# FFN bias added on GpSimd instead of TensorE, and FFN squares in place and two tiles wide, in a two-layer transformer kernel on one core

## The chip, the core and the metric

The kernel runs on one core of a Trainium2 chip. The metric is device time in microseconds. One execution of each kernel was also recorded by the hardware profiler. The engines are named as the profile names them: PE (TensorE, with PEld for its weight loads), ACT (ScalarE), DVE (VectorE), POOL (GpSimd) and SP (SyncE, which issues most DMAs here).

## The reference

Two layers with shared weights. Each is an attention and a feed-forward network (FFN), both behind a layer norm without parameters and with a residual. S = 2048 rows, D = 448, 16 heads of 28, F = 1792, all in bf16.

```python
def _A_ref(x, wqkv, wo):            # attention, 16 heads of 28, no mask
    q, k, v = split(x @ wqkv)
    p = softmax(q @ k.T * 28 ** -0.5)
    return (p @ v) @ wo

def _B_ref(x, w1, b1, w2, b2):      # FFN with a squared relu
    h = x @ w1 + b1
    r = where(h > 0, h, 0)
    return (r * r) @ w2 + b2

x = A_x
x = x + _A_ref(_layernorm(x), A_wqkv, A_wo)
x = x + _B_ref(_layernorm(x), B_w1, B_b1, B_w2, B_b2)
x = x + _A_ref(_layernorm(x), A_wqkv, A_wo)
x = x + _B_ref(_layernorm(x), B_w1, B_b1, B_w2, B_b2)
```

(Cut and abridged; `_layernorm` subtracts the mean and divides by the root of variance plus 1e-5.)

## The kernel before

All weights and x stay in SBUF for the whole run. Rows are worked on in **blocks** of two row tiles of 128 (256 queries); in layer 1 the last two blocks have one row tile each. The list `blocks` holds them.

**Attention.** For a block and a group of four heads, scores are computed in **units** of 512 columns: keys times queries, one head each, four heads side by side in PE's rows. There are 2048 units. `s_stream` takes up to three units at a time into one PSUM tile `sc` of three banks (L1154). There are two such tiles. `e_stream` takes the exponential of a whole tile on ACT (L1192), as bf16 into one of twelve `pt` tiles; an instruction has 1536 columns, or 1024 when the third unit is taken out. A unit that is taken out (`apart`, `a_unit`) has its exponential worked out by integer arithmetic: DVE reads the scores (L1214 or L1216), then three steps follow on POOL or DVE (`bent` L1263, `half` L1269, `whole` L1274) and one product on DVE (`close` L1278). In the other form, `a_whole` (L1232 to L1239), everything is on DVE. `p_stream` multiplies the results with the values (tile `oT`, L1380 and L1345). The denominators come out of the same product, and `norm_pair` or `norm_turn` divides by them.

**After attention** of a block, `chain(l, qb)` runs: the product with `wo` and the residual (`add_to_x`, L1513), the layer norm (statistics L648, a power on POOL at L673, normalized rows L772, transposes on PE L712, copy to `xnT` L724), and the FFN. The FFN's first product makes `mt` tiles of 512 columns in PSUM: two chunks of 128 hidden values by 256 rows, seven tiles to a block of two row tiles. `relu` (L1582 on ACT, L1584 on DVE) reads the tile and writes a buffer `r`, of which there are two (`rp`, resource `R_r`); `square` (L1589, L1591) reads `r` and writes the hidden values to their place (`hidden`: parts of `K_sb[1]`, `Q_sb`, `V_sb` or a tile `h`). While exponentials remain, DVE does both; after the last one ACT may take relus, and squares of the block before the last (`aside`). The second product, with `w2`, starts with a matmul of `one0` (ones in row 0 and zeros elsewhere) and `b2w` (the bias b2 in row 0), which adds the bias. DVE adds the sum to `x_sb` (L1513). The two blocks of one row tile at the end of layer 1 (`late`) do without that matmul: POOL adds b2 to their rows into a buffer `xf` (L1555), from a copy of b2 that a late DMA has put on all partitions. In layer 0 the block then makes its keys, values and queries for layer 1; in layer 1 the rows are stored (L1612).

**Order.** Nothing is ordered by the compiler. A `Planner` runs while the kernel is built: streams yield `Op`s with planned durations and dependencies, and the planner always issues the one that can start first, with priorities and rules on top. So the order on each engine is fixed at build time, by constants. `PACE` sets such constants anew at certain score tiles; the tables `FORCE` and `SKIP` name score tiles at which a unit must or must not be taken out. Where PE has room, a score tile's matmuls are repeated (`MORE`, `HOT`), and `heat` puts in matmuls without use (L1641), to keep PE's load up. An Op with `port=True` is planned so that POOL and DVE take turns: a POOL Op of that kind starts after DVE's, and the other way round.

Of the kernel before, what the change touches and what calls it, by code (L numbers as in the profile page):

```python
# [11 lines left out]
DT = mybir.dt  # L12
AF = mybir.ActivationFunctionType
ALU = mybir.AluOpType
P = 128
# [23 lines left out]
XMIN = 4  # L39
HELD = 0.14  # L40
# [105 lines left out]
FORCE = (22, 27, 31, 36, 64, 104, 108, 120, 122, 156, 162, 192, 196, 233, 235, 237, 254, 263, 287, 292, 301, 306,  # L146
         329, 341, 392, 408, 430, 445, 466, 501, 515, 553, 556, 567, 577, 593, 598, 602)
SKIP = (20, 29, 46, 135, 184, 195, 216, 222, 242, 262, 280, 282, 320, 321, 378, 388, 395, 404, 406, 409, 416, 418,
        433, 440, 446, 479, 500, 512, 526, 544, 574, 601, 609, 621, 622, 646, 652, 663)
PACE = {  # L150
    0: {'BUSY': 0.95, 'LOW': 0.7, 'CHUNK': 1, 'EV': 2.9, 'FAR': 6, 'KEEP': 5, 'LAG': 8, 'LEAD': 18, 'MARGIN': 3,
         'MORE': 3, 'PRE': 0.5, 'SLACK': 0.7, 'SPAN': 8, 'TB': 2.4, 'TB2': 2.4, 'V_AGE': 5, 'V_LAST': 3, 'V_PAST':
# [3 lines left out]
    8: {'LEAD': 12, 'BUSY': 0.9, 'PLIM': 2},  # L156
    16: {'SPAN': 11},
    24: {'LAG': 3},
    32: {'PLIM': 2.6, 'EV': 3.5},
    40: {'TB2': 3.0},  # L160
    42: {'BUSY': 0.95, 'CHUNK': 3, 'EV': 2.9, 'LAG': 8, 'LEAD': 18, 'MORE': 1, 'SPAN': 8, 'TB': 1.6, 'TB2': 2.4,
         'V_PRIO': 8.5},
    56: {'BUSY': 1.0, 'LAG': 3},
    64: {'NEAR': 9, 'ASIDE': 0.2, 'LADD': 0.1},
    72: {'V_AGE': 4},
    88: {'V_AGE': 3},
    112: {'C_PRIO': 1.2, 'HOLD': 5},
    120: {'LEAD': 10, 'LAG': 12, 'SPARE': 3, 'ASIDE': 2},
    128: {'TB': 2.0, 'MORE': 3},
    136: {'PRE': 1.2, 'MARGIN': 6},  # L170
    144: {'EPRIO': 4},
    152: {'CHUNK': 1, 'VGAP': 0},
    160: {'BUSY': 0.95, 'V_PRIO': 4, 'V_PAST': 3},
    168: {'RES': 1, 'C_PRIO': 2.1, 'LOW': 1.0},
    176: {'EV': 2.2, 'TB2': 2.0, 'LOW': 0.5},
    192: {'PORTP': 0.3, 'SOON': 0.6},
    200: {'CHUNK': 2, 'PRE': 0.3},
    208: {'PNEAR': 0.25, 'V_AGE': 6},
    216: {'NEAR': 3},
    248: {'EPRIO': 6},  # L180
    256: {'ASIDE': 0},
    264: {'MARGIN': 10},
    280: {'PORTP': 2},
    288: {'HOLD': 6},
    296: {'TB': 1.0, 'PNEAR': 0.15},
    304: {'SPAN': 6},
    312: {'BUSY': 1.0},
    320: {'LEAD': 12, 'MARGIN': 6},
    328: {'V_LATE': 6},
    336: {'LOW': 1.0},  # L190
    360: {'PNEAR': 0.05, 'TB': 2.4, 'V_LATE': 2.6, 'V_AGE': 3},
    368: {'C_PRIO': 1.6},
    376: {'PNEAR': 0.15, 'V_PRIO': 8.5},
    384: {'XMIN': 3, 'LEAD': 18},
    392: {'CHUNK': 3},
    400: {'KEEP': 6, 'ASIDE': 4, 'V_AGE': 6, 'BUSY': 0.9},
    408: {'PWAIT': 0.6, 'MORE': 1},
    424: {'RES': 2, 'BUSY': 1.0},
    440: {'HEAT': 0.6, 'WINDOW': 3.4, 'CHUNK': 2},
    456: {'V_AGE': 5, 'TB': 1.3},  # L200
    480: {'TB': 1.6, 'PORTP': 0.3, 'PLIM': 2},
    488: {'LADD': 0.2, 'HOLD': 4},
    496: {'MARGIN': 3, 'PNEAR': 0.35},
    504: {'PWAIT': 0.3},
    512: {'KEEP': 4, 'EV': 2.9},
    520: {'V_AGE': 4, 'C_PRIO': 1.2, 'HOLD': 5},
    528: {'PRE': 0.8},
    536: {'XMIN': 4, 'SPAN': 15, 'ASIDE': 2, 'PRE': 0.3},
    544: {'V_AGE': 5, 'EV': 2.2},
    552: {'PORTP': 1, 'LEAD': 12, 'FAR': 17, 'PRE': 0},  # L210
    560: {'V_LATE': 6, 'VGAP': 0.03},
    568: {'SPARE': 0, 'NEAR': 9},
    576: {'SOON': 1.5, 'PNEAR': 0.15},
    584: {'PLIM': 1.3, 'LAG': 3, 'V_WAIT': 3},
    592: {'KEEP': 6, 'V_LAST': 2.2},
    600: {'V_AGE': 8},
    608: {'EV': 1.3, 'LOW': 0.8},
    616: {'PRE': 1.2, 'BUSY': 0.95, 'V_PAST': 2, 'FAR': 6},
    624: {'LADD': 0.1, 'BUSY': 0.9},
    648: {'PRE': 0.5, 'SPAN': 20, 'EV': 3.5, 'ASIDE': 0.2},  # L220
    656: {'ASIDE': 1, 'SLACK': 0.4},
    672: {'SOON': 1, 'ASIDE': 0.2},
    680: {'SLACK': 0.7},
# [183 lines left out]
def kernel(  # L407
# [45 lines left out]
    R_r, R_xt, R_os, R_xn, R_on, R_rec = Res(2), Res(2), Res(NOS), Res(2), Res(2), Res(2)  # L453
# [96 lines left out]
    def loads():  # L550
# [28 lines left out]
        yield dma(b2w[0:1, :], B_b2.rearrange("(o d) -> o d", o=1), 30 * kb, ("b2",))  # L579
# [937 lines left out]
    def chain(l, qb):  # L1517
# [30 lines left out]
        if late:  # L1548
            b2b = flat_of(K_sb[0])[:, S:S + D]
            if ("b2b",) not in pl.tok:  # L1550
                yield dma(b2b, B_b2.rearrange("(o d) -> o d", o=1).to_broadcast([P, D]), 112 * 1024, ("b2b",))
            xf = flat_of(K_sb[0])[:, 2 * D * (late - 1):2 * D * late].bitcast(DT.float32)

            def add(e):
                nc.gpsimd.tensor_tensor(out=xf, in0=x_sb[:, t0, :], in1=b2b, op=ALU.add)  # L1555
# [6 lines left out]
        def hidden(i):  # L1562
            flat = lambda a: a.rearrange("p (f q) -> p f q", q=n)
            if l == 0 and i < 4:
                return (K_sb[1], Q_sb)[i // 2][:, 2 * (i % 2):2 * (i % 2) + 2, t0 * P:t0 * P + n]
            if l == 0 and i < 6:
                return flat(V_sb[1][:, t0:t0 + nt, :, :].rearrange("p t h r -> p (t h r)")[:, QB * (i - 4):QB * (i - 3)])
            if l == 0:
                return flat(hp.tile([P, QB], DT.bfloat16, name="h")[:, :])

            c = NFC * QR * (own_h.turn % 2) + QB * i
            return flat(V_sb[0][:, :, :, :].rearrange("p t h r -> p (t h r)")[:, c:c + QB])
        for f0 in range(0, NFC, pack):
# [3 lines left out]
            b = {}  # L1577

            def relu(e, t, b=b, w=w):
                r = b["r"] = rp.tile([P, QB], DT.bfloat16, name="r")  # L1580
                if e == "ACT":
                    nc.scalar.activation(out=r[:, 0:w], in_=t[:, 0:w], func=AF.Relu)  # L1582
                else:
                    nc.vector.tensor_scalar(out=r[:, 0:w], in0=t[:, 0:w], scalar1=0.0, scalar2=None, op0=ALU.max)  # L1584
            def square(e, b=b, w=w, f0=f0):
                r = b["r"][:, 0:w].rearrange("p (f q) -> p f q", q=n)
                b["h"] = h = hidden(f0 // pack)
                if e == "ACT":
                    nc.scalar.activation(out=h[:, 0:w // n, :], in_=r, func=AF.Square)  # L1589
                else:  # L1590
                    nc.vector.tensor_tensor(out=h[:, 0:w // n, :], in0=r, in1=r, op=ALU.mult)  # L1591

            def then(o, b=b, square=square):
                aside = not s_left and (l, qb) == (1, len(blocks[1]) - 2)
                b["s"] = Op("ACT" if aside else "DVE", 0.5 if aside else 0.42, square, deps=[o], rel=o, port=True)
# [99 lines left out]
```

## Time and profile before

| | us |
|---|---|
| median of 3 runs (lowest to highest) | 803.51 (803.49 to 803.66) |
| the profiled execution, own time | 803.48 |
| its span, first to last instruction | 801.7 |
| first exponential starts | 9.28 |
| last exponential ends | 787.08 |

The profile gives a busy time for each engine, groups of instructions by line and shape (count, busy time, mean duration, and the idle time ahead of them with what ended it), a timeline with start and duration, and busy times in windows. Durations on ACT include a start-up and drain that overlap with the instruction next to them, and matmuls overlap too, so busy times of ACT and PE cannot be added up from single durations; the distance between two starts is the measure there. The granted TensorE clock was 1.00 throughout.

### The profile page before, as it was taken

Reading aid. Unit: us, or ns where it says so; the run is one execution under the profiler, and the core shown is the slowest. Engines: PE = TensorE matmul, PEld = TensorE weight load, DVE = VectorE, ACT = ScalarE, POOL = GpSimd, SP = SyncE. Lnnn points to the kernel's source line nnn. Section 1 sums busy time; section 2 is a strip of 40 time slices with the busy share of each in tenths; the row PEclk is TensorE's granted clock in tenths of the full one; section 3 lists DMA queues with packets and bytes.
Section 4 is the critical chain, followed back from the end, with each engine's and each line's share of the span. In section 5 each row is a group of like instructions: output and inputs, shape, how many; then the busy total and the mean of one; then the engine's idle time right before and its main releaser. Section 6 shows DMA issues by size and latency. Waiting matters only on the chain.

```text
span 801.7 us, 29246 instructions
## 1 busy us (share of the span) xinstructions
PE 778.7 (97%) x12242; PEld 417.6 (52%) x12242; DVE 744.8 (93%) x1818; ACT 789.4 (98%) x702; POOL 454.7 (57%) x717
## 2 busy tenths in 40 slices
PE   9999989999999999999999999989999999999998
PEld 6555545544555545555455545445454544545666
DVE  8999999999999999999999998999999999989564
ACT  8999999999999999999999999999999999999995
POOL 3346777657676664544566657657665566654200
PEclk9999999999999999999999999999999999999999
DMA  9300010000000000000000000011100000000100
GB/s 250 86 2 2 5 34 23 17 16 16 17 3 16 16 16 16 3 16 15 2 3 2 3 2 2 15 32 30 33 11 22 21 28 21 22 23 9 27 8 19
DMA packets 32480, 18.13 MB, mean 23 GB/s; under 512 B 17818, under 2 KB 31899, under 8 KB 32348
## 3 DMA queue, kind: packets, MB, share of 16 engines
q1 hardware_dynamic: 32204, 16.16, 7.4%
q8 instruction: 95, 1.56, 0.8%
q14 instruction: 37, 0.30, 0.1%
q10 hardware_dynamic: 144, 0.11, 0.0%
HBM read 13.98 MB, written 2.06 MB: 20 GB/s over the span
## 4 chain that ended last, share of the span: by engine, by line
PE 41%; ACT 33%; DVE 17%; issue 8%; DMA 0%; POOL 0%; ACTq 0%; DVEq 0%
ACT pt L1192 33%; PE mt L809 19%; PE sc L1154 12%; PE oT L1380 7%; DVE pt L1216 2%; DVE r L1584 2%; PE oT L1345 1%; DVE pt L1214 1%; DVE V_sb L1591 1%; DVE K_sb L1278 1%; DVE v_c L1278 1%; DVE v_c L1216 1%; PE tp L712 1%; DVE x_sb L1513 1%; PE sc L809 1%
## 5 line engine op out<-in xcount | busy, mean ns | idle before, releaser
L1192 ACT ACTIVATE pt<-sc 128x1536 bf16<-128x1536 f32 (+1 forms) x683 | 776.6, 1292 | 1.2 <-PE sc L1154 0.9
L1154 PE MATMUL sc<-Q_sb,K_sb 32*128 32x256 bf16 (+1 forms) x4652 | 279.6, 265 | 15.7 <-ACT pt L1192 13.5
L1154 PEld LDWEIGHTS <-K_sb 32*128 32x128 bf16 x4652 | 101.1, 92 | 186.3 <-issue 118.3
L1380 PE MATMUL oT<-pt,V_sb 128*32 128x256 bf16 (+1 forms) x4000 | 167.8, 268 | 0.5 <-DVE Q_sb L828 0.3
L1380 PEld LDWEIGHTS <-V_sb 128*32 128x32 bf16 x4352 | 101.5, 96 | 45.3 <-issue 35.9
L809 PE MATMUL mt<-xnT,w 128*128 128x256 bf16 (+1 forms) x904 | 119.6, 270 | 0.9 <-DVE xnT L724 0.2
L1274 POOL TENSOR_SCALAR pt<-pt 128x512 int16<-128x512 int8 x131 | 83.9, 642 | 39.9 <-ACT pt L1192 5.7
L809 PEld LDWEIGHTS <-w 128*128 128x128 bf16 x952 | 78.0, 98 | 35.2 <-issue 26.4
L1216 DVE TENSOR_SCALAR pt<-sc 128x512 int16<-128x512 f32 x132 | 89.8, 684 | 2.3 <-PE sc L1154 1.6
L1584 DVE TENSOR_SCALAR r<-mt 128x512 bf16<-128x512 f32 (+1 forms) x107 | 73.0, 682 | 3.8 <-PE mt L809 3.4
L673 POOL TENSOR_TENSOR rstd<-mv,mhalf 128x2 f32<-128x2 f32 (+1 forms) x34 | 25.4, 747 | 76.4 <-DVE mv L676 48.2
L809 PE MATMUL mt<-w,V_sb 128*128 128x448 bf16 (+2 forms) x288 | 66.5, 345 | 0.0
L1274 POOL TENSOR_SCALAR v_c<-v_c 128x512 int16<-128x512 int8 x64 | 42.8, 668 | 24.5 <-DVE V_sb L1269 4.3
L1269 POOL TENSOR_SCALAR v_c<-pt 128x512 f16<-128x512 uint8 x57 | 37.8, 663 | 31.9 <-DVE K_sb L1263 5.8
L1513 DVE TENSOR_TENSOR x_sb<-x_sb,mt 128x448 bf16<-128x448 bf16 x61 | 37.4, 612 | 12.9 <-PE mt L809 12.6
L1216 DVE TENSOR_SCALAR v_c<-sc 128x512 int16<-128x512 f32 x69 | 46.6, 682 | 0.7 <-PE sc L1154 0.6
L648 DVE BATCH_NORM_STATS2 st<-x_sb 128x6 f32<-128x448 bf16 x63 | 38.9, 619 | 0.7 <-DMA x_sb<-in_A_x_dram 0.5
L809 PEld LDWEIGHTS <-V_sb 128*128 128x128 bf16 x302 | 25.4, 98 | 24.4 <-issue 10.0
L1345 PE MATMUL oT<-v_c,V_sb 128*32 128x256 bf16 (+1 forms) x298 | 35.0, 273 | 0.0
L1591 DVE TENSOR_TENSOR V_sb<-r 128x512 bf16<-128x512 bf16 x70 | 29.2, 421 | 3.0 <-ACT r L1582 2.8
L1274 POOL TENSOR_SCALAR K_sb<-K_sb 128x512 int16<-128x512 int8 x39 | 25.3, 650 | 11.2 <-DVE v_c L1278 2.4
L1269 POOL TENSOR_SCALAR K_sb<-pt 128x512 f16<-128x512 uint8 x35 | 23.9, 682 | 13.2 <-DVE pt L1216 4.3
(219 smaller groups left out, 1254.0 us busy)
## 6 DMA issues: line engine op xcount, KB each, us to landing
rec<-scr SPq DMA_DIRECT2D x54, 128.0 KB
out_dram<-x_sb SPq DMA_DIRECT2D x15, 112.0 KB
x_sb<-in_A_x_dram SPq DMA_DIRECT2D x7, 224.0 KB
w<-in_B_w_dram SPq DMA_DIRECT2D x1, 1568.0 KB
w<-in_B_w_dram SPq DMA_DIRECT2D x1, 1344.0 KB
dn<-oT_sb SPq DMA_DIRECT2D x54, 4.0 KB
V_sb<-in_A_wqkv_dram SPq DMA_DIRECT2D x4, 168.0 KB
scr<-dn SPq DMA_DIRECT2D x27, 8.0 KB
```

The costliest lines, as they stand in the source:

```text
L648: nc.vector.bn_stats(out=box["st"][:, :], in_=x_sb[:, t0 + j, :] if src is None else src())
L809: nc.tensor.matmul(box["t"][:, c0:c0 + n], lhsT=lhsT() if callable(lhsT) else lhsT, rhs=rhs, start=a, stop=b)
L1154: nc.tensor.matmul(dst[k][:, i * nt * P:(i + 1) * nt * P], lhsT=K_sb[l][rows, g, (kb + i) * P:(kb + i + 1) * P], rhs=Q_sb[rows, g, t0 * P: ...
L1192: t = nc.scalar.activation(out=pt[:, 0:n], in_=gbuf[gi]["sc"][:, 0:n], func=AF.Exp, scale=float(np.log(2.0)) * 2.0 ** -FRAC)
L1216: t = nc.vector.tensor_scalar(out=z.bitcast(DT.int16), in0=src, scalar1=2.0, scalar2=EXP_BIAS, op0=ALU.mult, op1=ALU.add)
L1269: on(e).tensor_scalar(out=box["f"], in0=gbuf[gi]["z"].bitcast(DT.uint8).rearrange("p (n t) -> p n t", t=2)[:, :, 0], scalar1=2.0 ** -9, sc ...
L1274: on(e).tensor_scalar(out=gbuf[gi]["z"].bitcast(DT.int16), in0=gbuf[gi]["z"].bitcast(DT.int8).rearrange("p (n t) -> p n t", t=2)[:, :, 1], ...
L1345: nc.tensor.matmul(box["t"][DHP * hh:DHP * hh + DHP, 0:n], lhsT=V_sb[l][:, kb + i, 4 * g + hh, :], rhs=gbuf[gi]["x2"][:, i * n:(i + 1) * n ...
L1380: nc.tensor.matmul(box["t"][DHP * hh:DHP * hh + DHP, 0:n], lhsT=V_sb[l][:, tb, 4 * g + hh, :], rhs=p, start=begin and j < G, stop=close an ...
L1513: nc.vector.tensor_tensor(out=x_sb[:, tb, lo:hi], in0=x_sb[:, tb, lo:hi] if src is None else src[:, lo:hi], in1=t[:, 0:hi - lo], op=ALU.add)
L1584: nc.vector.tensor_scalar(out=r[:, 0:w], in0=t[:, 0:w], scalar1=0.0, scalar2=None, op0=ALU.max)
L1591: nc.vector.tensor_tensor(out=h[:, 0:w // n, :], in0=r, in1=r, op=ALU.mult)
```

## The change

Three things are changed.

1. **Bias.** For blocks of two row tiles, after the layer norm's transposed rows have been copied (`ends`), one POOL instruction adds b2 to both row tiles of `x_sb` in place, and the second FFN product has no bias matmul any more, but waits for that instruction. b2 is loaded to all 128 partitions of `b2w` by the opening loads; the two late blocks use this copy, and their own load goes.
2. **Squares.** Relu writes its result to the place of the hidden values; the `r` buffers and their resource are gone. Square works in place, for blocks of two row tiles on two FFN tiles at once (1024 columns): tiles 0 and 1, 2 and 3, 4 and 5; tile 6 is squared alone. Blocks of one row tile are squared tile by tile.
3. **Pace.** `FORCE`, `SKIP` and all of `PACE` are other numbers (only the first of them are shown).

```diff
+BIAS = 1
+BDUR = 1.15
+BPRIO = 4.5
+TWO = 1
-FORCE = (22, 27, 31, 36, 64, 104, 108, 120, 122, 156, 162, 192, 196, 233, 235, 237, 254, 263, 287, 292, 301, 306,
-         329, 341, 392, 408, 430, 445, 466, 501, 515, 553, 556, 567, 577, 593, 598, 602)
+FORCE = (31, 42, 59, 63, 82, 87, 265, 289, 302, 346, 355, 370, 397, 455, 685)
...
-    R_r, R_xt, R_os, R_xn, R_on, R_rec = Res(2), Res(2), Res(NOS), Res(2), Res(2), Res(2)
+    R_xt, R_os, R_xn, R_on, R_rec = Res(2), Res(NOS), Res(2), Res(2), Res(2)
...
-        yield dma(b2w[0:1, :], B_b2.rearrange("(o d) -> o d", o=1), 30 * kb, ("b2",))
+        yield dma(b2w[:, :] if BIAS else b2w[0:1, :], B_b2.rearrange("(o d) -> o d", o=1).to_broadcast([P, D]) if BIAS else B_b2.rearrange("(o d) -> o d", o=1), 30 * kb, ("b2",))
...
-            b2b = flat_of(K_sb[0])[:, S:S + D]
-            if ("b2b",) not in pl.tok:
-                yield dma(b2b, B_b2.rearrange("(o d) -> o d", o=1).to_broadcast([P, D]), 112 * 1024, ("b2b",))
+            b2b = b2w[:, :]
...
-            xb = Op("POOL", 1.2, add, deps=[a, ("b2b",)], port=True)
+            xb = Op("POOL", 1.2, add, deps=[a, ("b2",)], port=True)
             pl.spawn(3.3, iter([xb]))
+        elif BIAS:
+            def biased(e):
+                nc.gpsimd.tensor_tensor(out=x_sb[:, t0:t0 + nt, :], in0=x_sb[:, t0:t0 + nt, :],
+                                        in1=b2w[:, :].unsqueeze(1).to_broadcast([P, nt, D]), op=ALU.add)
+            bias = Op("POOL", nt * BDUR, biased, deps=[("b2",), *ends], port=True)
+            pl.spawn(BPRIO, iter([bias]))
...
+            second = TWO and nt == 2 and i0 % 2 == 1
+            lone = not TWO or nt != 2 or f0 + pack >= NFC
...
-                r = b["r"] = rp.tile([P, QB], DT.bfloat16, name="r")
+                if not second:
+                    b["h"] = hidden(i0, 2 - lone)
+                k = w // n
+                h = b["h"][:, second * pack:second * pack + k, :]
+                src = t[:, 0:w].rearrange("p (f q) -> p f q", q=n)
                 if e == "ACT":
-                    nc.scalar.activation(out=r[:, 0:w], in_=t[:, 0:w], func=AF.Relu)
+                    nc.scalar.activation(out=h, in_=src, func=AF.Relu)
                 else:
-                    nc.vector.tensor_scalar(out=r[:, 0:w], in0=t[:, 0:w], scalar1=0.0, scalar2=None, op0=ALU.max)
+                    nc.vector.tensor_scalar(out=h, in0=src, scalar1=0.0, scalar2=None, op0=ALU.max)
...
+                h = b["h"][:, 0:b["n"], :]
                 if e == "ACT":
-                    nc.scalar.activation(out=h[:, 0:w // n, :], in_=r, func=AF.Square)
+                    nc.scalar.activation(out=h, in_=h, func=AF.Square)
                 else:
-                    nc.vector.tensor_tensor(out=h[:, 0:w // n, :], in0=r, in1=r, op=ALU.mult)
+                    nc.vector.tensor_tensor(out=h, in0=h, in1=h, op=ALU.mult)
...
-                relu, 0.685, [*([] if split else ends), ("w1",)], True, post=[then], acq=R_r, across=split)
+                relu, 0.685, [*([] if split else ends), ("w1",)], True, post=[then], across=split)
...
-                    [(0, hi - lo, ([] if late else [(one0[:, :], b2w[:, lo:hi])])
+                    [(0, hi - lo, ([] if late or BIAS else [(one0[:, :], b2w[:, lo:hi])])
...
-                    [*([] if own_deps else [hacts[-1][2]]), ("w2",), xb if late else ("b2",)],
+                    [*([] if own_deps else [hacts[-1][0]["s"]]), ("w2",), xb if late else bias if BIAS else ("b2",)],
```

167 lines of the change are left out of this document (82 added, 85 removed).

## The prediction

> **What bounds the kernel now.** First the page's opening and its chain of waits.
>
> ```profile
> span 801.7 us, 29246 instructions
> ...
> PE 778.7 (97%) x12242; PEld 417.6 (52%) x12242; DVE 744.8 (93%) x1818; ACT 789.4 (98%) x702; POOL 454.7 (57%) x717
> ...
> PE 41%; ACT 33%; DVE 17%; issue 8%; DMA 0%; POOL 0%; ACTq 0%; DVEq 0%
> ```
>
> ACT is busy 789.4 of 801.7 us. PE's 97% is softer, because its matmuls overlap. To see what ACT does, take the groups by line with shapes kept apart, then single exponentials from the timeline (start, duration).
>
> ```profile
> L1192 ACT ACTIVATE pt<-sc 128x1536 bf16<-128x1536 f32 x345 | 490.1, 1504 | 0.6 <-PE sc L1154 0.5
> L1192 ACT ACTIVATE pt<-sc 128x1024 bf16<-128x1024 f32 x338 | 338.4, 1076 | 0.6 <-PE sc L1154 0.4
> ```
>
> ```profile
> 9.28 1.45 ACT L1192 ACTIVATE pt<-sc 128x1536 bf16<-128x1536 f32 x1
> ...
> 716.28 1.08 ACT L1192 ACTIVATE pt<-sc 128x1024 bf16<-128x1024 f32 x1
> 720.79 1.15 ACT L1192 ACTIVATE pt<-sc 128x1024 bf16<-128x1024 f32 x1
> 749.79 1.45 ACT L1192 ACTIVATE pt<-sc 128x1536 bf16<-128x1536 f32 x1
> 783.04 1.78 ACT L1192 ACTIVATE pt<-sc 128x1536 bf16<-128x1536 f32 x1
> 785.84 1.24 ACT L1192 ACTIVATE pt<-sc 128x1024 bf16<-128x1024 f32 x1
> ```
>
> The run has three parts: 9.28 us of opening, the exponentials from 9.28 to 785.84 + 1.24 = 787.08, and a tail of 14.6 us. In the middle ACT waits 0.6 + 0.6 us by the groups, but that hides something: one exponential starts before the last has drained. From 749.79 to 783.04 lie 25 starts of the wide form, 1.330 us apart; from 716.28 to 720.79 five of the narrow one, 0.902 apart. So 345 x 1.330 + 338 x 0.902 = 763.7 us would be enough for what took 777.8. About **14 us are small bubbles**, spread over the whole stretch. They are all that a better order can win there; the rest is a sum of ACT instructions. How busy the other engines are meanwhile is read in windows.
>
> ```profile
> core 0: us, PE busy (x) PEld busy (x) DVE busy (x) ACT busy (x) POOL busy (x), PEclk, DMA share, GB/s
> ...
> 500.00:600.00 100.00, 94.25 (x1461) 47.03 (x1452) 99.26 (x247) 99.80 (x92) 65.63 (x102) 1.00 0.09 24
> ...
> 700.00:787.00 87.00, 85.82 (x1780) 50.66 (x1779) 64.27 (x158) 87.00 (x71) 25.96 (x39) 1.00 0.06 17
> ```
>
> DVE is as full as ACT in the middle and has room only at the end; POOL has a third of its time free; the granted clock is 1.00.
>
> **The change part by part.** Counts of the changed kernel are from the compiled order of its instructions beside the old one.
>
> *Exponentials.* 2048 units of 512 columns go to ACT in threes or twos, or one by one to DVE. DVE takes 337 before and 335 after, so ACT gets two more: still 683 instructions, now 347 wide and 336 narrow. By the two forms a unit is 1.330 - 0.902 = 0.43 us: **+0.86 us**, on the path. This term is nearly certain.
>
> *Matmuls removed.* 30 bias matmuls go, and fillers that only keep PE busy fall from 30 to 13; repeated score matmuls rise by 138.
>
> ```profile
> L809 PE MATMUL mt<-b2w,one x30: 349/363/363, 161.7 to 778.8; 128*128 128x448 bf16 x30
> ...
> 774.46 0.36 PE L809 MATMUL mt<-b2w,one 128*128 128x448 bf16 x1
> 774.66 0.35 PE L809 MATMUL mt<-w,V_sb 128*128 128x448 bf16 x1
> ```
>
> The first row has the shortest, median and longest of the 30 and their first and last start. In the timeline the next matmul follows 0.20 us later: 47 x 0.20 = 9.4 us off PE. The 138 repeats run in 23 rounds of six, four side by side; at 256/448 of 0.20 a matmul, a round is 0.17 us and all of them 4 us. PE sheds about 5 us, off the path except where a score arrives late.
>
> *Squares and the rest of DVE.*
>
> ```profile
> L1591 DVE TENSOR_TENSOR V_sb<-r 128x512 bf16<-128x512 bf16 x69 | 28.9, 423 | 3.0 <-ACT r L1582 2.8
> L1591 DVE TENSOR_TENSOR V_sb<-r 128x256 bf16<-128x256 bf16 x1 | 0.3, 284 | 0.0
> L1584 DVE TENSOR_SCALAR r<-mt 128x512 bf16<-128x512 f32 x106 | 72.6, 685 | 3.8 <-PE mt L809 3.4
> L1269 DVE TENSOR_SCALAR v_c<-v_c 128x512 f16<-128x512 uint8 x5 | 2.1, 421 | 0.0
> L1263 DVE TENSOR_SCALAR v_c<-pt 128x512 int16<-128x512 int16 x21 | 6.0, 286 | 0.0
> ```
>
> No square of 1024 is in the trace. From 256 to 512 columns adds 139 ns, so 1024 should take 423 + 2 x 139 = 701 against 846 for two (bounds: 562, if the next 512 cost 139; 846, no gain). 45 pairs x 0.145 = 6.5 us saved. Also from the order: 21 conversions at 0.42 and 6 like them leave DVE for POOL (-11.3); 23 halvings at 0.29 come the other way (+6.7); four relus come over from ACT (+2.7); two units fewer and odd ones -2. DVE: **-10 us**, about 1.4%, in an engine that is full. Relu now writes its final place, so its wait for one of two r buffers goes; the next wait there is for the matmul, which the relu row already names (3.4 of its 3.8 us).
>
> *The bias on GpSimd.*
>
> ```profile
> L1555 POOL TENSOR_TENSOR K_sb<-x_sb,K_sb 128x448 f32<-128x448 bf16 x2 | 2.3, 1128 | 1.3 <-DVE xn L772 1.0 <-DVE r L1584 0.3
> L1274 POOL TENSOR_SCALAR pt<-pt 128x512 int16<-128x512 int8 x131 | 83.9, 642 | 39.9 <-ACT pt L1192 5.7 <-DVE v_c L1263 4.0 <-DVE K_sb L1278 2.8
> L1591 DVE TENSOR_TENSOR Q_sb<-r x16: 406/418/791, 133.8 to 461.3; 128x512 bf16<-128x512 bf16 x16
> ```
>
> 15 adds over two row blocks, each twice 1.128 = 2.26 us: 34 us. At 0.65 the moved conversions and halvings change POOL by (18 + 3 - 26) x 0.65 = -3 us. POOL goes to about 485 us of 803, and has room. Queued behind a bias in POOL's order are conversions whose results PE waits for; and PE's second FFN matmul waits for the bias. The bias is ready to start when the normalized rows are turned, seven FFN tiles earlier (7 relus are 4.8 us of DVE alone, more than 2.26), so I cost that wait at nothing; if it were not covered, PE would stand up to 2.26 us at each. The third row (shortest, median, longest) shows a square that took 791 ns where 418 is usual; while POOL works, some DVE instructions with SBUF inputs wait. Here the Trainium skill, "SBUF — State Buffer", "Who interferes with whom", says that the port pair of DVE and GpSimd is an exclusive lock held for a whole instruction. By that a bias could hold DVE for 2.26 us where a conversion holds it 0.65; the long square agrees with it. The cost by row is between 0 (the planner gives the port in turns) and 2.26 a piece, 34 us in all, of DVE's time; I take 0 net here, nearest to the medians, and keep the other end as a rival. The bias vector is now loaded to all rows at the end of the opening loads, and SP's late second load goes; the first bias matmul was at 161.7 us, so I cost both at nothing (up to a load's time, 1 or 2 us once, if the first reader came early).
>
> *The pace, hence the bubbles.* From the order, I summed the PE work between one group of score matmuls and the next (the pitch above, in proportion to columns; 32-wide ones four at a time). Gaps above 0.9 us, where the next score can miss its narrow exponential, fall from 104 to 92, and what they hold above 0.9 from 21.0 to 18.7 us, by 11%. Of 14 us of bubbles that would be 1.5; some are drain at the opening, which is unchanged, so I take **-1.0** (bounds -6 and +6: a new order can win or lose nearly half).
>
> *The tail.* Instructions after the last exponential, from the timeline.
>
> ```profile
> 788.48 0.29 DVE L1462 TENSOR_TENSOR oTn<-oT,rec 128x128 bf16<-128x128 f32 x1
> ...
> 789.23 0.63 DVE L648 BATCH_NORM_STATS2 st<-mt 128x6 f32<-128x448 f32 x1 [0.46 <-PE mt L809]
> ...
> 793.96 0.60 ACT L1582 ACTIVATE r<-sc 128x512 bf16<-128x512 f32 x1 [2.38 <-PE sc L809]
> ...
> 796.91 0.28 DVE L1591 TENSOR_TENSOR V_sb<-r 128x256 bf16<-128x256 bf16 x1
> 797.84 0.42 DVE L1513 TENSOR_TENSOR x_sb<-K_sb,mt 128x256 bf16<-128x256 f32 x1 [0.64 <-issue]
> 798.94 0.35 DVE L1513 TENSOR_TENSOR x_sb<-K_sb,mt 128x192 bf16<-128x192 f32 x1 [0.68 <-PE mt L809]
> ```
>
> In the new order a relu of 0.69 stands between oTn and the statistics: 788.77 + 0.69 = 789.46 instead of 789.23, +0.23. In the last block, ACT did the relus while DVE squared; now DVE does relu and square in turn three times, then an add, then the last square. From about 794.1: 3 x (0.69 + 0.42) + 0.61 + 0.28 = 4.2, so 798.3 where it was 797.2; two 256-column and 14 192-column matmuls (1.4 us) and an add of 0.35, with hand-overs, still follow, so the last add ends near 800.3, not 799.3. I take **+0.9** for the tail (bounds 0, if the first matmuls hide it, and +1.3).
>
> **Sum.** The profiled run took 803.48 us, 1.78 more than its span, and 0.03 less than the median, 803.51. 803.48 + 0.86 + 0.9 - 1.0 = 804.2.
>
> **The rivals.**
>
> *The bias holds DVE (slower).* For it: DVE at 99.26 of 100 us, the 791 ns square. Against it: medians at 418 beside a POOL that is busy 65 of 100 us. If each bias costs DVE half its hold, 15 x 1.13 = 17 us, less the 10 saved, 7 are left; half of it reaching ACT by late oT and late scores is 3.5, and the 1.0 is not won: 803.48 + 0.86 + 0.9 + 3 = about 808.5. It decides from 10/15 = 0.67 us per bias on. The Trainium skill's lock (the page above) is the same mechanism; by it alone the 34 us less 10 would be the far end.
>
> *Lighter DVE and PE shrink the bubbles (faster).* For it: 10 us off a full DVE and 5 off PE, r's buffers gone, fewer full gaps. Against: ACT got two units more, not fewer. A fall by 5 of the 14 us gives 803.48 + 1.76 - 5 = 800.2.
>
> *Nothing is won in the middle.* Bubbles as before: 805.2, the upper part of my forecast.
>
> **How the numbers follow.** The forecast, 804.2 with its own range 801.8 to 806.0, has 0.46: 0.33 within 0.2% (801.9 to 805.1, about what a measurement of this kernel can tell from no change), 0.11 above, 0.02 below. The bias rival has 0.26, all slower; the bubble rival 0.28, all faster. So faster 0.30, same 0.33, slower 0.37. The range 800.0 to 808.6 reaches both rivals' times and leaves out the far halves of their spreads, about 2 in 10.
>
> **What would show it.** Exponentials: 347 and 336, starts 1.330 and 0.902 apart, so 764.5 us net; the stretch from the first to the last of them less this is the bubbles: 13 by the forecast, 9 or less for the faster rival, 16 or more for the slower. A square of 1024 near 0.70 us; a bias near 2.26 with DVE's medians unchanged; many squares above 0.8 us beside it would speak for the lock. The tail should be 15.5 us. I am wrong if the bubbles move by more than 3 us either way, or if the tail is shorter than before.

## The result

The changed kernel takes 807.15 us in the median of 6 runs (806.85 to 808.19), the kernel before 803.52 (803.49 to 803.66) on the same chip. The ratio is 1.0048, with a 95% interval of 1.0035 to 1.006: slower by 0.45%, 3.6 us. The profiled execution took 807.25 us for a span of 805.5.

The profile after, first the page's opening, its row of granted clocks and its chain, as they were shown of before.

```profile
span 805.5 us, 29336 instructions
...
PE 779.3 (97%) x12339; PEld 420.3 (52%) x12339; DVE 746.3 (93%) x1770; ACT 788.4 (98%) x699; POOL 487.2 (60%) x727
...
PEclk9999999999999999999999999998999999999999
...
ACT 42%; PE 39%; issue 9%; DVE 8%; DMA 1%; POOL 1%; SPq 0%; ACTq 0%; DVEq 0%; POOLq 0%
```

ACT is busy for the same 788 to 789 us; the run is longer by what ACT waits. And one digit of the clock row is 8, where before had 9 throughout. The groups of exponentials and the ends of their stretch, from the groups with shapes apart and from the timeline:

```profile
L1186 ACT ACTIVATE pt<-sc 128x1536 bf16<-128x1536 f32 x347 | 495.2, 1503 | 2.0 <-PE sc L1148 1.3 <-ACT pt L1186 0.3
L1186 ACT ACTIVATE pt<-sc 128x1024 bf16<-128x1024 f32 x336 | 339.3, 1083 | 1.5 <-PE sc L1148 1.3
```

```profile
9.23 2.94 ACT L1186 ACTIVATE pt<-sc 128x1536 bf16<-128x1536 f32 x2
...
542.91 3.71 ACT L1186 ACTIVATE pt<-sc 128x1024 bf16<-128x1024 f32 x3 [0.18 <-PE sc L1148]
547.41 2.59 ACT L1186 ACTIVATE pt<-sc 128x1536 bf16<-128x1536 f32 x2 [0.80 <-PE sc L1148]
550.58 1.94 ACT L1186 ACTIVATE pt<-sc 128x1024 bf16<-128x1024 f32 x2 [0.58 <-PE sc L1148]
...
784.95 5.11 ACT L1186 ACTIVATE pt<-sc 128x1536 bf16<-128x1536 f32 x4
```

ACT's wait for scores grew from 1.2 us in all to 3.5, of which 0.18 + 0.80 + 0.58 = 1.6 us lie between 542 and 551 us. The three parts of the run are then, in us:

| | before | after | difference |
|---|---|---|---|
| opening, to the first exponential | 9.28 | 9.23 | -0.05 |
| exponentials without bubbles (x 1.330, x 0.902) | 763.7 | 764.6 | +0.9 |
| bubbles in the stretch (777.8 and 790.06 - 9.23 = 780.83) | 14.1 | 16.2 | +2.1 |
| tail | 14.62 | 15.44 | +0.8 |
| span | 801.7 | 805.5 | +3.8 |

I then added up, exponential by exponential, how much later each one started than the pitch allows, in both traces. The bubbles differ most in two places; elsewhere they are a little more here and less there (-0.6 at exponentials 500 to 560, +0.5 at 360 to 440). The two places are: at exponentials 469 to 475 (near 545 us) 0.11 before and 1.89 after, and at 90 to 95 (near 117 us) 0.18 before and 0.90 after.

**The first place is a slow clock.** The windows around it, 10 and 20 us wide, of the changed kernel and then of the kernel before (columns: window, its length, busy time and count of PE, PEld, DVE, ACT, POOL, then the granted clock):

```profile
540.00:550.00 10.00, 8.98 (x106) 4.24 (x100) 8.19 (x23) 8.90 (x8) 4.57 (x7) 0.66 0.10 22
515.00:535.00 20.00, 15.54 (x263) 7.88 (x260) 19.48 (x53) 20.00 (x20) 10.58 (x17) 1.00 0.12 31
```

```profile
540.00:550.00 10.00, 9.81 (x156) 5.59 (x155) 9.76 (x24) 10.00 (x11) 6.70 (x12) 1.00 0.11 30
515.00:535.00 20.00, 17.54 (x300) 8.56 (x300) 19.75 (x53) 20.00 (x19) 11.78 (x19) 1.00 0.14 36
```

From 541.4 to 548.2 us, 6.83 us long, TensorE runs at half its clock, and 0.66 is the mean over the window. In this time a round of 12 score matmuls takes 1.20 us (third row), at full clock 0.61 (first row). The second row shows the longest wait of PE ahead of it, 0.73 us:

```profile
533.74 0.61 PE L1148 MATMUL sc<-Q_sb,K_sb 32*128 32x256 bf16 x12 [0.52 <-ACT pt L1186]
...
540.95 0.40 PE L1148 MATMUL sc<-Q_sb,K_sb 32*128 32x256 bf16 x6 [0.73 <-ACT pt L1186]
...
542.19 1.20 PE L1148 MATMUL sc<-Q_sb,K_sb 32*128 32x256 bf16 x12
```

From 515 to 535 us PE was busy for 15.54 of 20 us, where the kernel before had 17.54. Part of the difference are the fillers of `heat`. Here is their group between 510 and 545 us, by their weight loads, before and then after (shortest, median and longest duration, first and last start):

```profile
L1641 PEld LDWEIGHTS <-ident x23: 95/96/99, 513.5 to 543.6; 128*128 128x128 bf16 x23
```

```profile
L1653 PEld LDWEIGHTS <-ident x10: 95/96/115, 518.5 to 543.3; 128*128 128x128 bf16 x10
```

In the old `PACE` an entry at score tile 440 raises the load that `heat` aims at; the new `PACE` has no such entry. The slow clock was no accident of the profiled execution: all six runs of the changed kernel had a mean clock of 0.996 or 0.998. The three at 0.998 took 806.85 to 807.05 us, the three at 0.996 took 807.25 to 808.19.

The Trainium skill, "TensorE: Matmul & The Clock Gate", Part 1, says that the clock has two states, full and half, and falls to half after an idle window of about 3.4 us. The two states and the length agree (6.83 is two windows). The word idle doesn't: PE never waited longer than 0.73 us in the 27 us ahead of the fall, it was only thinly used. How thin is too thin is read from all the traces at the end.

### The profile page after: what moved, and what is told of

The parts are those of the page before. It is cut to its first block, busy times and chain, and to the rows that moved or that the text cites. A ratio compares the mean times of both kernels' runs of the same rounds, so it can differ in the third digit from the quotient of the medians.

```text
span 805.5 us, 29336 instructions
## 1 busy us (share of the span) xinstructions
PE 779.3 (97%) x12339; PEld 420.3 (52%) x12339; DVE 746.3 (93%) x1770; ACT 788.4 (98%) x699; POOL 487.2 (60%) x727
## 4 chain that ended last, share of the span: by engine, by line
ACT 42%; PE 39%; issue 9%; DVE 8%; DMA 1%; POOL 1%; SPq 0%; ACTq 0%; DVEq 0%; POOLq 0%
ACT pt L1186 42%; PE mt L803 17%; PE sc L1148 12%; PE oT L1374 7%; PE oT L1339 2%; DVE pt L1210 1%; PE tp L706 1%; DVE V_sb L1592 1%; PE sc L803 1%; DVE V_sb L1599 1%; DMA rec<-scr 1%; DVE K_sb L1208 0%; DVE K_sb L1210 0%; DMA scr<-dn 0%; DVE K_sb L1272 0%
## 5 line engine op out<-in xcount | busy, mean ns | idle before, releaser
L1148 PE MATMUL sc<-Q_sb,K_sb 32*128 32x256 bf16 (+1 forms) x4790 | 285.4, 266 | 18.5 <-ACT pt L1186 15.4
L1148 PEld LDWEIGHTS <-K_sb 32*128 32x128 bf16 x4790 | 106.9, 92 | 191.0 <-issue 125.4
L1374 PEld LDWEIGHTS <-V_sb 128*32 128x32 bf16 x4352 | 100.9, 96 | 44.5 <-issue 35.6
L1268 POOL TENSOR_SCALAR pt<-pt 128x512 int16<-128x512 int8 x111 | 71.9, 648 | 34.5 <-ACT pt L1186 3.5
L1210 DVE TENSOR_SCALAR pt<-sc 128x512 int16<-128x512 f32 x111 | 75.7, 684 | 6.8 <-PE sc L1148 5.3
L803 PE MATMUL mt<-w,V_sb 128*128 128x448 bf16 (+1 forms) x288 | 68.4, 351 | 0.2
L1268 POOL TENSOR_SCALAR v_c<-v_c 128x512 int16<-128x512 int8 x77 | 51.1, 665 | 20.1 <-DVE K_sb L1272 1.7
L1210 DVE TENSOR_SCALAR v_c<-sc 128x512 int16<-128x512 f32 x77 | 52.2, 681 | 1.7 <-PE sc L1148 1.5
L1592 DVE TENSOR_SCALAR V_sb<-mt 128x512 bf16<-128x512 f32 x69 | 46.7, 679 | 5.8 <-PE mt L803 5.4
L1263 POOL TENSOR_SCALAR v_c<-v_c 128x512 f16<-128x512 uint8 x45 | 31.2, 694 | 21.9 <-DVE v_c L1257 2.7
L1339 PEld LDWEIGHTS <-V_sb 128*32 128x32 bf16 x688 | 24.8, 96 | 10.9 <-issue 9.7
```

What stands on the lines that cost most here:

```text
L803: nc.tensor.matmul(box["t"][:, c0:c0 + n], lhsT=lhsT() if callable(lhsT) else lhsT, rhs=rhs, start=a, stop=b)
L1148: nc.tensor.matmul(dst[k][:, i * nt * P:(i + 1) * nt * P], lhsT=K_sb[l][rows, g, (kb + i) * P:(kb + i + 1) * P], rhs=Q_sb[rows, g, t0 * P: ...
L1210: t = nc.vector.tensor_scalar(out=z.bitcast(DT.int16), in0=src, scalar1=2.0, scalar2=EXP_BIAS, op0=ALU.mult, op1=ALU.add)
L1263: on(e).tensor_scalar(out=box["f"], in0=gbuf[gi]["z"].bitcast(DT.uint8).rearrange("p (n t) -> p n t", t=2)[:, :, 0], scalar1=2.0 ** -9, sc ...
L1268: on(e).tensor_scalar(out=gbuf[gi]["z"].bitcast(DT.int16), in0=gbuf[gi]["z"].bitcast(DT.int8).rearrange("p (n t) -> p n t", t=2)[:, :, 1], ...
L1339: nc.tensor.matmul(box["t"][DHP * hh:DHP * hh + DHP, 0:n], lhsT=V_sb[l][:, kb + i, 4 * g + hh, :], rhs=gbuf[gi]["x2"][:, i * n:(i + 1) * n ...
```

## The experiments

My theory was: the bubbles are the clock's, and the clock is the fillers'; the tail is the relus on DVE; the bias and the lighter DVE change nothing. The rivals: the bias holds the port that DVE shares with GpSimd; DVE's time still decides; the rest is the new pace as such. Other parts of the change can't be undone one by one, since each makes another plan; so all but one run (ASIDE, below) leave the order on the engines as it is and change what stands at one place of it. The medians of the kernel before on the chips used were 803.59 to 803.72 us, and its clock was 1.00 in each of its 33 runs there.

### More matmuls ahead of the slow clock

```diff
-                for i in list(range(4)) * (again + 1):
+                for i in list(range(4)) * (again + 1 + (440 <= gi < 470 and o.room > 0.3)):
```

> The changed kernel, with its order kept, but 16 more rounds of repeated score matmuls (96 matmuls) at the score tiles 440 to 469 where PE has room, ahead of the 6.83 us in which the trace shows the TensorE clock at one half. Theory (PE was too little used there, the clock was halved, and the late scores cost ACT some 2.2 us): the granted clock is 1.000, the bubbles of the exponentials 469 to 474 go, 805.0 us. Rival (the bubbles there come from late results of DVE or GpSimd, and the half clock comes along with them): the bubbles stay and the added matmuls make them longer, 807 us or more.

806.62 us (805.74 to 807.17), ratio 1.0036 (1.0024 to 1.0049). The clock is 1.00 in all five runs, and the bubbles at 469 to 475 fall from 1.89 to 0.09. But the added rounds made other scores late: 440 to 459 +0.35, 476 to 499 +0.79, and 560 to 639 +0.54. So the bubbles are 16.1 us in all, almost as many as the 16.2 of the changed kernel. The clock part of the theory holds, its time of 805.0 doesn't: the price of the remedy ate most of the gain.

### The kernel before without its fillers there

```diff
                 def junk(e):
+                    if 430 <= gi < 480:
+                        return
```

> The kernel before, order kept, without the 23 filler matmuls between 513 and 544 us (they write nothing that is used). Theory: the same stretch of thin PE work then halves the clock here too, for several us, without any bias or square being touched: 805.5 us, granted clock 0.996 to 0.998. Rival (it is the bias on GpSimd or the new order, not the fillers): clock 1.000 and 803.5 us, or a little less.

806.22 us (806.08 to 807.93), ratio 1.0038 (1.0024 to 1.0052): the kernel before loses 2.5 us by losing 23 matmuls that compute nothing. The clock row of its page, and the windows:

```profile
PEclk9999999999999999999999999889999999999999
```

```profile
515.00:535.00 20.00, 15.73 (x238) 8.12 (x235) 17.24 (x48) 17.69 (x16) 10.20 (x16) 0.66 0.12 30
```

The clock is halved for 13.65 us from 515.1 on, and the bubbles at 440 to 459 grow from 0.25 to 2.96. All five runs had a clock below 1 (0.989 to 0.994). This shows the cause from the other side, with nothing of the change in the kernel.

### Rounds of scores only where PE has room

```diff
+                for i in list(range(4)) * (again + 1 + {447: 1, 450: 1, 451: 1, 455: 1, 462: 1,
+                                                        466: 2, 467: 2, 468: 1}.get(gi, 0)):
```

> The changed kernel, order kept, with only 10 added rounds of repeated scores, at the score tiles 447, 450, 451, 455, 462 and 466 to 468, where the trace shows PE idle and the score ready 0.27 us or more ahead of its exponential. Theory (the half clock costs 2 us; what the 16 rounds of the first try won they lost again, because other score tiles came late): granted clock 1.000, bubbles near 13 us, 805.1 us. Rival (the clock is not what costs): 806.6 us or more, as with the 16 rounds.

806.04 us (805.81 to 807.65), ratio 1.0035 (1.0023 to 1.0047), span 804.0, bubbles 14.6. Ten added rounds bring PE's busy time from 515 to 535 us from 15.54 to 16.23 of 20 us, and the clock in the profiled run stays at 1.00:

```profile
515.00:535.00 20.00, 16.23 (x289) 8.70 (x289) 19.39 (x53) 20.00 (x20) 10.47 (x17) 1.00 0.12 31
540.00:550.00 10.00, 8.95 (x169) 5.33 (x162) 9.84 (x27) 9.91 (x10) 6.16 (x9) 1.00 0.12 25
```

Against the changed kernel that is 1.1 us less, of the 2.1 of bubbles; the 805.1 and the 13 us of the theory were not reached. Three of the five runs kept the clock and took 805.81 to 806.04 us; the other two had 0.997 and took 807.24 and 807.65. Within one kernel, then, the runs with a slow clock are 1.2 us or more behind those without. Where the clock fell in these two isn't recorded.

### No bias on GpSimd

The 15 additions of b2 are left out, so the blocks of two row tiles miss it.

```diff
             def biased(e):
+                return
```

> The changed kernel, order kept, without the 15 GpSimd instructions that add the bias (so the FFN's bias is left out in all blocks of two row tiles). In the changed kernel four DVE instructions beside a bias took 1.97, 1.80, 1.26 and 0.96 us where 0.29, 0.24, 0.42 and 0.68 are usual, 4.4 us of waiting for the port. Theory (these waits fall where DVE has some slack, and the bubbles around them are no longer than in the kernel before): 0 to 1 us faster, 806.2 to 807.2 us. Rival (DVE is the hidden bound and the port is what the change cost): 3 to 5 us faster, 803 us.

807.42 us (806.73 to 810.07), ratio 1.0051 (1.0039 to 1.0063): no gain. What the biases cost elsewhere can be read from the busy row of its page:

```profile
PE 779.2 (97%) x12339; PEld 420.2 (52%) x12339; DVE 742.2 (92%) x1770; ACT 788.2 (98%) x699; POOL 458.4 (57%) x712
```

POOL loses 28.8 us (15 x 1.9), DVE 4.1 us, that is 0.27 us for each bias. DVE is held a little, and this doesn't reach ACT: the clock was halved for 6.83 us here too, and the bubbles are 16.2 us as with the bias.

### The bias twice

Each bias is added twice, so the result has b2 once too often.

```diff
+                nc.gpsimd.tensor_tensor(out=x_sb[:, t0:t0 + nt, :], in0=x_sb[:, t0:t0 + nt, :],
+                                        in1=b2w[:, :].unsqueeze(1).to_broadcast([P, nt, D]), op=ALU.add)
```

> The changed kernel, order kept, with each bias instruction issued twice in a row (so the bias is added twice in blocks of two row tiles): 15 x 1.88 = 28 us more on GpSimd, and the port is held 3.76 us at a time. Theory (GpSimd has a third of its time free, but what is queued behind the second add comes 1.9 us late, and DVE waits for the port): 2 to 6 us slower, 809 to 813 us, with more long DVE instructions. Rival (GpSimd's time is free and the port does not matter): 807 us.

821.15 us (819.03 to 822.02), ratio 1.0213 (1.02 to 1.0226), bubbles 27.4.

```profile
PE 780.4 (95%) x12339; PEld 419.8 (51%) x12339; DVE 761.5 (93%) x1770; ACT 791.8 (97%) x699; POOL 517.2 (63%) x742
```

The second bias, for which the plan keeps no turn at the port, costs 14 us of time, more than either side expected, and 15 us of DVE's (761.5 against 746.3), 1.0 us for each. So a bias can hold DVE for far longer than the 0.27 us of the planned one. That the turn given by the planner makes this difference fits, but no run takes the turn away. Nor does this run tell how much of the 14 us is the port and how much POOL's later conversions.

### Each wide square as two

```diff
-                    nc.vector.tensor_tensor(out=h, in0=h, in1=h, op=ALU.mult)
+                    for a in range(0, b["n"], pack):
+                        nc.vector.tensor_tensor(out=h[:, a:min(a + pack, b["n"]), :], in0=h[:, a:min(a + pack, b["n"]), :],
+                                                in1=h[:, a:min(a + pack, b["n"]), :], op=ALU.mult)
```

> The changed kernel with each square of two tiles issued as two instructions of 512 columns, in the same place of DVE's order. By durations, 45 x (0.84 - 0.68) = 7 us more DVE work. Theory (DVE's load is not what bounds the stretch, and part of each start-up is hidden by the next instruction): DVE busy rises by about 4 us, time rises by 0 to 0.8 us. Rival (DVE is the hidden bound, so what the wide squares save is worth its full time): 7 us more, 814 us.

814.39 us (813.34 to 817.99), ratio 1.0141 (1.0122 to 1.0161), bubbles 22.7, spread over the whole stretch. DVE is busy for 756.8 us, 10.5 more, not the 7.5 that 45 x (0.846 - 0.68) would add. The squares of 512 columns now take 0.52 us in the mean where 0.42 is usual: 27 of the 108 took 0.69 to 1.26 us, each of them beside an instruction on POOL, which fits waits for the port. The rival held: the 10.5 us added to DVE in this order cost 7.2 us of time.

### Wide squares of 32 columns

The 45 wide squares work on 32 columns, so the rest of the hidden values isn't squared.

```diff
+                    if b["n"] * n > QB:
+                        h = h[:, 0:1, 0:32]
```

> The changed kernel, order kept, with each of the 45 wide squares cut to 32 of its 1024 columns (so most of the hidden values are not squared): some 45 x 0.5 = 22 us less on DVE. With the squares in halves, 7 us more on DVE had cost 7 us. Theory (the order is fixed, so DVE time that is saved against the plan is not spent on more exponentials; ACT has its 765 us of instructions anyway): 1 to 4 us faster, from fewer bubbles, 803 to 806 us. Rival (DVE time counts in full in both directions): 10 us faster or more, below 797 us.

808.03 us (806.84 to 809.59), ratio 1.0054 (1.0042 to 1.0066): nothing won, though theory and rival both expected a gain. The windows from 100 to 700 us, of the changed kernel and then of this run:

```profile
100.00:700.00 600.00, 581.13 (x8928) 302.97 (x8922) 574.58 (x1342) 597.23 (x533) 393.91 (x583) 0.99 0.06 15
```

```profile
100.00:700.00 600.00, 580.35 (x8948) 303.26 (x8943) 560.46 (x1343) 597.78 (x534) 385.05 (x583) 1.00 0.06 15
```

DVE is lighter by another 14 us of 600, and ACT is as busy as it was: the spare time becomes idle time on DVE. A slow clock doesn't hide a gain: it was halved for 3.41 us (from 523.5 on) where the changed kernel had 6.83, and the bubbles of this run are 15.6 us, of which 1.3 more than in the changed kernel lie at exponentials 440 to 459. Units are given to DVE or ACT when the kernel is built; what isn't planned in isn't used. Taken with the run before: in this fixed order, DVE's time cost most of itself when it grew and was worth nothing when it shrank.

### The tail's relus given to ACT by the plan

```diff
-    680: {'ASIDE': 0},
+    680: {'ASIDE': 0.2},
```

> The changed kernel with ASIDE at score tile 680 set from 0 to 0.2, so that ACT takes the last block's relus again, as in the kernel before; the order differs only at the end. Theory (DVE does relu and square in turn, which makes the tail 0.8 us longer): tail 14.6 us instead of 15.4, 806.3 us. Rival (relus on ACT and squares on DVE hand over at each tile, which costs as much): 807.2 us or up to 0.9 more.

810.1 us (807.5 to 810.98), ratio 1.0073 (1.006 to 1.0087): the expectation fell. The planner moved more than the relus. On the timeline of this run, POOL and DVE:

```profile
795.83 1.03 POOL L1547 TENSOR_TENSOR K_sb<-x_sb,b2w 128x448 f32<-128x448 bf16 x1
```

```profile
795.83 1.17 DVE L766 TENSOR_SCALAR xn<-x_sb,mv,rstd 128x448 bf16<-128x448 bf16 x1
...
804.46 0.42 DVE L1507 TENSOR_TENSOR x_sb<-K_sb,mt 128x256 bf16<-128x256 f32 x1 [2.29 <-issue]
805.56 0.35 DVE L1507 TENSOR_TENSOR x_sb<-K_sb,mt 128x192 bf16<-128x192 f32 x1 [0.68 <-PE mt L803]
805.94 0.62 DVE L1507 TENSOR_TENSOR x_sb<-K_sb,sc 128x448 bf16<-128x448 f32 x1
```

The late block's addition on POOL now starts with DVE's normalized rows, which take 1.17 us for 0.39, and the add of the last block but one has become the very last instruction. Tail 17.2 us. The clock was halved twice besides (near 116 and 543 us).

### The tail's relus on ACT in the order as it is

On top of the ten placed rounds, four relus of 512 columns are issued on ACT instead of DVE, and nothing else moves.

```diff
-                if e == "ACT":
+                if e == "ACT" or (l, qb, i0) in ((1, len(blocks[1]) - 2, 1), (1, len(blocks[1]) - 1, 0), (1, len(blocks[1]) - 1, 1), (1, len(blocks[1]) - 1, 2)):
```

> The kernel with ten placed repeat rounds (806.04 us, tail 15.56 us, no half clock), but in the tail four relus of 512 columns run on ACT instead of DVE: one of the last block but one (it stands between the product with rec and the statistics) and three of the last block (they alternate with the squares). Nothing else moves; PE, POOL and SP have the same order. Theory (the tail got longer because DVE does relu and square in turn): the tail comes back to that of the kernel before, 14.6 to 14.9 us, and the time to about 805.3. Rival (PE's chain of 46 matmuls after the last transposed rows sets the end, and DVE's order is hidden): tail 15.3 or more, time as it was, 806.0. In neither case is the kernel before (803.5) reached: two units more on ACT (0.86 us) and a different set of bubbles are left.

805.59 us (805.03 to 806.34, 9 runs, all at clock 1.00), ratio 1.0026 (1.0016 to 1.0036), span 803.3. The last exponential ends at 788.20, so the tail is 15.1 us, between theory and rival, 0.4 less than with the relus on DVE (15.4 in the changed kernel and with ten placed rounds, where the expectation says 15.56). The changed kernel's last block, then this run's, DVE on the timeline:

```profile
794.23 0.39 DVE L766 TENSOR_SCALAR xn<-x_sb,mv,rstd 128x448 bf16<-128x448 bf16 x1
795.38 0.42 DVE L718 COPY xnT<-sc 128x512 bf16<-128x512 bf16 x1 [0.77 <-PE sc L706]
797.03 0.69 DVE L1592 TENSOR_SCALAR V_sb<-sc 128x512 bf16<-128x512 f32 x1 [1.23 <-PE sc L803]
797.75 0.42 DVE L1599 TENSOR_TENSOR V_sb<-V_sb 128x512 bf16<-128x512 bf16 x1
798.10 0.68 DVE L1592 TENSOR_SCALAR V_sb<-mt 128x512 bf16<-128x512 f32 x1
...
800.75 0.28 DVE L1599 TENSOR_TENSOR V_sb<-V_sb 128x256 bf16<-128x256 bf16 x1
```

```profile
792.25 0.39 DVE L766 TENSOR_SCALAR xn<-x_sb,mv,rstd 128x448 bf16<-128x448 bf16 x1
793.51 0.42 DVE L718 COPY xnT<-sc 128x512 bf16<-128x512 bf16 x1 [0.87 <-PE sc L706]
795.79 0.42 DVE L1599 TENSOR_TENSOR V_sb<-V_sb 128x512 bf16<-128x512 bf16 x1 [1.85 <-ACT V_sb L1590]
796.68 0.43 DVE L1599 TENSOR_TENSOR V_sb<-V_sb 128x512 bf16<-128x512 bf16 x1 [0.47 <-ACT V_sb L1590]
...
798.45 0.28 DVE L1599 TENSOR_TENSOR V_sb<-V_sb 128x256 bf16<-128x256 bf16 x1
```

Relu and square in turn take 800.75 - 795.38 = 5.37 us from the turned rows to the last square; with ACT's help it is 4.94. The kernel before needed 4.94 as well (791.97 to 796.91). What is left of the tail lies ahead of that: normalized rows to turned rows take 1.26 us here and 0.92 before (791.05 to 791.97). In both kernels the transposes stand behind eight matmuls of the second product on PE. In the new order 24 matmuls of the first product lie between the product with `wo` and these eight, where the kernel before has 18, and PE works through them without a pause. Six more at a distance of 0.056 us are 0.34 us, all of the difference. That is read from the two traces; no run tests it.

### One exchange on DVE, for the place near 117 us

The product `oTn`, which waits for a DMA, is put behind the ready product that followed it.

```diff
+        if (l, qb, g) == (0, 1, 2):
+            pl.later = m
...
+                if o is self.later:
+                    self.held, self.gap = o, 2
```

> As the run with the tail's relus on ACT, and one pair of neighbours on DVE is exchanged, near 114 us: the product oTn, which waited for the DMA that brings rec, stands behind a product that was ready (0.34 us of work) instead of ahead of it. Theory (the late exponential at 117 us comes from DVE standing behind that DMA, so that the oT read and PE's next oT matmul are late): the bubble of exponentials 90 to 95, 0.66 us in the run with placed repeats, falls by about 0.3, and the time by as much, to about 805.0. Rival (the scores there are late for another reason, such as PE's own work): the bubble stays between 0.6 and 0.9 and the time does not move.

805.95 us (805.62 to 807.69), ratio 1.0034 (1.0022 to 1.0047); the bubble at 90 to 95 grew to 1.10. As a remedy it failed in this execution, in which the DMA came later than in any other; the bubble is outside what theory and rival expected. But that tells the cause, since the order up to there was the same in the runs before it. One row from each of three kernels: the changed one, the run with the relus on ACT, and this one.

```profile
114.64 0.69 DVE L1498 TENSOR_TENSOR oTn<-oT_sb,rec 128x512 bf16<-128x512 f32 x1 [0.66 <-DMA rec<-scr]
```

```profile
114.22 0.69 DVE L1498 TENSOR_TENSOR oTn<-oT_sb,rec 128x512 bf16<-128x512 f32 x1 [0.17 <-DMA rec<-scr]
```

```profile
115.17 0.69 DVE L1509 TENSOR_TENSOR oTn<-oT_sb,rec 128x512 bf16<-128x512 f32 x1 [0.74 <-DMA rec<-scr]
```

The bubbles that go with these starts are 0.90, 0.41 and 1.10. The wait of DVE stands in the brackets. In the first two rows the bubble is this wait plus 0.24 us, and so it is in six other executions with this order and full clock at the place (waits 0.27, 0.42, 0.57, 0.63, 0.77, 0.87; bubbles 0.51, 0.66, 0.80, 0.87, 1.01, 1.11). The kernel before had no wait there and 0.18 us of bubble. The later the DMA lands, the later `oTn`, the read of oT behind it, and the score that PE owes to ACT. That it is this wait is shown by the range of landings, not by the exchange.

## Why the prediction came out as it did

The time lies in the upper part of the range, on the side that had a chance of 0.37; the likeliest case, 804.2 with its own range 801.8 to 806.0, didn't come. The cause was none of the rivals'. That 807.15 still lies inside the range of 800.0 to 808.6 is luck in part: my own forecast ended at 806.0, and the range went further only for the rival of the bias, which didn't happen. (That rival's sum, 803.48 + 0.86 + 0.9 + 3, gives 808.2, or 808.7 with its own 3.5, not 808.5.) Point by point:

- **Exponentials, +0.86: right.** 347 and 336, so 764.6 us net.
- **PE sheds 5 us, costed at nothing: the step that failed.** I counted the fillers (30 to 13) as load taken off PE, and covered a change of PE by "a score arrives late" only. Not how much PE had to do, but how little, decided: where 23 fillers between 510 and 545 us had kept the clock, 10 didn't, and 6.83 us at half clock cost 1.8 us of bubbles. The new pace took away what the old one had put there. The run without fillers in the kernel before shows it (+2.5), the ones with more rounds show it back (-0.5 and -1.1). The sentence "the granted clock is 1.00" stood in the prediction, but not what holds it there.
- **Squares and DVE, -10: right as a sum of durations, and worth nothing.** All durations on DVE added up fell by 9.1 us (876.9 to 867.8). The wide square took 0.68 us for 0.70 forecast. Rows of the two changed operations:

```profile
L1599 DVE TENSOR_TENSOR V_sb<-V_sb x40: 283/678/691, 146.0 to 800.7; 128x1024 bf16<-128x1024 bf16 x29, 128x512 bf16<-128x512 bf16 x10, 128x256 bf16<-128x256 bf16 x1
...
L1552 POOL TENSOR_TENSOR x_sb<-x_sb,b2w x15: 1872/1879/2172, 132.5 to 749.8; 128x896 bf16<-128x896 bf16 x15
```

  But neighbours on DVE overlap, and its busy time counts an overlap once: it fell by 6.2 us from 100 to 700 us (580.8 to 574.6) and rose by 8.1 from 700 us on (70.7 to 78.8), so over the whole run it is 746.3 us for 744.8. Units on DVE stayed at the 335 of the new plan, so nobody got the time; the run with squares of 32 columns shows that even 14 us more buy nothing.
- **Bias, net 0: right.** 1.88 us for 2.26, 0.27 us of DVE's time for each, far below the 0.67 from which the rival was to decide, and no gain without it. With 16 us of bubbles the result had the mark that I had set for this rival, yet it came from elsewhere: a sum can't tell causes, the place of the bubbles can.
  One instruction beside a bias shows the hold all the same, first POOL's row, then DVE's (a conversion for which 0.29 us is usual):

```profile
399.50 2.17 POOL L1552 TENSOR_TENSOR x_sb<-x_sb,b2w 128x896 bf16<-128x896 bf16 x1
```

```profile
399.85 1.97 DVE L1257 TENSOR_SCALAR v_c<-pt 128x512 int16<-128x512 int16 x1
```

  It ends at 401.82, just behind the bias, which ends at 401.67. The lock of the Trainium skill ("SBUF — State Buffer", "Who interferes with whom") agrees with this.
- **Bubbles, -1.0: wrong, +2.1.** The term came from counting PE's work in the order at full clock, and such a count can't see a clock. Without the slow clock the bubbles are 14.6 (placed rounds) and 14.3 (with the relus on ACT), against 14.1 before: the term would have been between +0.2 and +0.5, and the new pace wins nothing even so. (With the 16 rounds of the first try they were 16.1 at full clock, because other scores came late.) In this rest, up to 0.7 us near 117 us is a DMA that lands too late for its new place.
- **Tail, +0.9: right, +0.8, by the mechanism named for half of it.** The four relus on DVE are worth 0.4. Relu ahead of the statistics cost 0.12 instead of 0.23 (from `oTn` to the statistics 0.87 us, 791.55 to 792.42, where 0.75 were needed); the later transposes weren't foreseen.

So 803.48 + 0.86 + 0.8 + 2.1 = 807.2. That this meets the profiled 807.25 proves nothing, since the bubbles are what is left of the time; what shows the cause is where they lie and the runs that move them. The best version found, placed rounds with the tail's relus on ACT, stands at 805.59, still 0.26% above the kernel before. In its profiled execution, 805.03, two units more on ACT (0.9 us), half a microsecond of tail and 0.2 of bubbles are left of the change; why the median lies another half a microsecond higher is open.

## What to carry to other kernels

When a change takes work off TensorE that computes nothing, ask first what that work was for: look at the clock row before any other, and search for the thinnest stretch of a few microseconds (3.41 here); a mean over 20 us can look the same with and without a fall. An engine that was freed in an order fixed at build time gained nothing here, while time added to it cost most of itself. And a DMA's landing time is a range: an instruction planned into the middle of that range is late in some executions.

## What the runs showed of the hardware

- The half clock came in lengths of 3.41, 6.83 and 13.65 us, multiples of one length. The two falls of one execution (the run with ASIDE at 0.2, at 116.47 and 543.13 us) lie 125 such lengths apart. This reads like a grid of 3.41 us on which the clock is decided and which lies elsewhere in each execution; it would explain why falls at 541.4, 523.5 and 116.5 us are found in kernels whose matmuls have the same order up to there.
- The 3.41 us right ahead of a fall tell more than the mean over 20 us. Three of the eight falls inside the traced runs, with the windows that end there: the changed kernel, the kernel before without its fillers, and the squares in halves (columns as above).

```profile
537.96:541.37 3.41, 2.25 (x50) 1.23 (x51) 3.38 (x9) 3.41 (x4) 2.41 (x4) 1.00 0.25 77
```

```profile
511.73:515.15 3.42, 2.14 (x48) 1.18 (x47) 3.42 (x7) 3.42 (x5) 2.88 (x5) 1.00 0.04 6
```

```profile
389.32:392.73 3.41, 1.95 (x50) 1.24 (x48) 3.41 (x8) 3.09 (x4) 2.15 (x4) 1.00 0.00 0
```

Ahead of all eight PE was busy for 1.95 to 2.27 of 3.41 us. Over 20 us ahead of the second of these falls it was busy for 18.02, more than the 16.23 and 17.54 with which the clock stayed full; and with the squares in halves, a stretch with the same 15.54 of 20 us as in the changed kernel (519.5 to 539.5 us) passed at full clock.
- Four traces (the kernel before, more matmuls, placed rounds, the tail's relus on ACT) have no 3.41 us from 15 to 780 us, wherever one begins, in which PE is busy for less than about 2.3 us, and none of them has a fall. In the changed kernel the thinnest such stretch has 2.00 us. A stretch like that doesn't always bring a fall: the run with the exchange on DVE has one of 2.04 us (from 113.06 on) and kept the clock there. Nor is busy time the whole measure: counted in steps of 3.41 us from their own falls, the run with squares in halves has windows of 2.11 and 2.25 us without a fall, and the run with the bias twice has three of 1.94 to 2.25.
- 6.83 us of half clock cost 1.8 us, and 13.65 us some 2.7 (the bubbles of exponentials 440 to 459), far less than the slow time itself.
- DVE came to the product that needs `rec` at 113.98 to 114.10 us in nine executions with the same order up to there, and waited for the transfer for 0.17 to 0.89 us, so that it started anywhere from 114.22 to 114.92. SP had issued the transfer between 109.43 and 109.83, so part of the range may lie in the issue.
- A late transfer and the clock can meet: in the run with ASIDE, DVE's wait was 0.89 us, PE was busy for 2.01 of the 3.41 us up to 116.47, the clock fell there, and the bubbles at 90 to 95 were 2.60 us.
